# Zeroing in parts on two engines, weights issued first, and dense layers of half-filled tiles on their 64 rows, in a recurrent-memory transformer kernel

## The chip, the cores and the metric

The kernel runs on one core of one Trainium2 chip. The metric is the device time of one execution in microseconds (us). Every timing set runs the kernel before and the other kernel on the same chip. All runs quoted here are of the state that the measurement calls fast.

The engines are called TensorE (PE in the profile; PEld are its weight loads), VectorE (DVE), ScalarE (ACT), GpSimd (POOL) and SyncE (SP). PEclk is the TensorE clock that was granted, as a share of full speed.

## The reference, cut to what matters

```python
x = A_x                                                    # 2048 rows of 512
x = x + _A_ref(_layernorm(x), A_mem0, Wq, Wk, Wv, Wo, 32)  # A: attention over segments with a memory
x = x + _B_ref(_layernorm(x), w1, w2)                      # B: relu(x @ w1) @ w2, 512 -> 1376 -> 512
x = x + _A_ref(_layernorm(x), A_mem0, Wq, Wk, Wv, Wo, 32)
x = x + _B_ref(_layernorm(x), w1, w2)

def _A_ref(x, mem0, Wq, Wk, Wv, Wo, seg_len):
    mem = mem0                                             # 8 rows
    for s in range(64):                                    # one segment of 32 rows after the other
        h = concat([mem, xs])                              # 40 rows
        # q, k, v of 32 heads of 128; masked softmax; o = (p v) Wo
        mem = o[:, :8]                                     # the next segment needs this
        outs.append(o[:, 8:])
```

The memory makes the 64 segments of a layer A sequential. The second layer A can follow the first at a distance.

## The kernel before: the parts that matter

The kernel walks 68 *steps*. In step k it computes segment k of the first layer A and segment k-4 of the second one side by side. After every second step a *pair* (two segments, 64 rows) is finished. Pair j holds the first layers' pair j in rows 0 to 63 of a 128-row tile and the second layers' pair j-2 in rows 64 to 127, and one dense layer works on the whole tile. So of the 34 pairs, pairs 0 and 1 have only the upper half filled, and pairs 32 and 33 only the lower half. The kernel before computes all 128 rows for them all the same.

All work is described as operations with an engine, an estimated cost, what they read and what they write. A list scheduler in the kernel puts them in an order, which is then fixed. The constants RULE and AHEAD shift the priorities in that scheduler. Some operations may go to either of two engines.

```python
def load_weights():
    for i, part in enumerate(("v0", "v2", "q0", "k0", "q2", "k2", "o0", "o2")):
        ...                                    # nc.gpsimd.dma_start of 2 MB each
        plan.op(POOL, 1.0, dma, w=[("W", c, pc), ("W", c, pc + 1)], lag=0.0)

def load_dense():                              # w1 by SyncE, w2 by GpSimd, after the weights ("loaded")
    ...
    plan.op(eng, t, dma, r=["loaded"], w=[w, *[("values", g, p) ...]], lag=10.0)
    # w1_sb and w2_sb hold the values of four groups (EARLY = 4) until these are stored to DRAM (vh)

    # ... prepare():
    def zero_rest():                           # one operation, VectorE alone
        for t in (*Pt, *p_PT.tiles, V0, vw, *p_x.tiles, *p_ox.tiles, *p_xr.tiles, *p_h.tiles):
            nc.vector.memset(t[:], 0.0)

def dense_layer(x, rows):
    xnT = layernorm(x, rows, p_xm)             # VectorE statistics, GpSimd power, VectorE norm, TensorE transpose
    hT = p_h.buf()
    for fb in range((NFC + 3) // 4):           # NFC = 11 chunks of 128 of the 1376 columns
        ...
            for fi, fc in enumerate(fcs):      # first product: 44 weight tiles, 128 columns each
                for c4 in range(NC4):
                    across(cols, hp[0:fs, fi * 128:(fi + 1) * 128], w1_sb[:, c4, fc * 128:fc * 128 + fs],
                           xnT[:, c4, :], start=(c4 == 0), stop=(c4 == NC4 - 1))
        ...                                    # relu into hT
    yp = b_fill.buf()
    ...                                        # second product: 11 matmuls of 512 columns
            across(cols, yp[:, :], hT[0:fs, fc, :], w2_sb[0:fs, fc, :], start=(fc == 0), stop=(fc == NFC - 1))
    return yp

    # ... finish_pair(j), for rows of the second layers:
        def add1():                            # VectorE: the result; then SyncE stores it
            nc.vector.tensor_tensor(out=ob[PR:2 * PR, :], in0=x[PR:2 * PR, :], in1=yp[PR:2 * PR, :], op=ALU.add)

# ... late_values(g): values of 16 rows of each segment of group g, early for g = 1 to 4
        def put():
            nc.sync.dma_start(out=vh[g][:], in_=room[:, :, :])      # 512 KB

prepare()
load_weights()
prepare_group(0)
...
load_dense()
for k in range(nsteps):
    ...                                        # step_values, queries_keys, scores, attend, project
    if k % 2 and k // 2 < NP + D2:
        finish_pair(k // 2)
```

Of the kernel before, what the change touches and what calls it, by code (L numbers as in the profile page):

```python
# [29 lines left out]

RULE = (0.045, 0.734, 51.008, 20.581)
AHEAD = {
    "attend.ev": 0.03, "attend.mm": -1.07, "dense_layer.mm": -0.93, "dense_layer.relu": 1.18,
    "dense_layer.relu_last": -2.98, "finish_pair.add": 2.93, "finish_pair.add0": -0.42, "finish_pair.store": -6.14,
    "finish_pair.turn": 2.99, "finish_pair.widen": 5.86, "late_values.cp": 0.58, "late_values.put": -0.12,
    "layernorm.eps": 0.15, "layernorm.keep": -5.93, "layernorm.norm": 1.95, "layernorm.power": 0.74,
    "layernorm.stats": 0.87, "layernorm.turn": -30.83, "load_dense.dma1": -1.99, "load_dense.dma2": 0.39,
    "load_group.get": 2.78, "load_group.load": -0.5, "load_weights.dma": -3.92, "make_ident": -5.09,
    "make_mask": -0.88, "place_values.dma": -1.35, "prep_x.cp": 3.85, "prepare.get_memory": 0.75,
    "prepare.get_x": 0.11, "prepare.keep": -10.8, "prepare.place": 4.03, "prepare.turn": 5.85,  # L40
    "prepare.zero_banks": 2.29, "prepare.zero_columns": 5.96, "prepare_group.load": 6.09, "prepare_group.put": 0.52,
    "project.ev": 4.4, "project.first": 7.37, "project.mm": -1.19, "queries_keys.ev": 4.38, "queries_keys.mm": -0.14,
    "scores.block": 0.27, "scores.exp": 0.85, "scores.keep": -13.15, "scores.mul": -5.63, "scores.recip": 1.98,
    "scores.sub": -8, "scores.top": 0.05, "scores.total": 20.81, "scores.turn": 1.11, "values.ev": 0.12,
    "values.mm*": -37.11,
}
# [260 lines left out]
def kernel(  # L307
# [74 lines left out]
    def load_weights():  # L382



        for i, part in enumerate(("v0", "v2", "q0", "k0", "q2", "k2", "o0", "o2")):
            c, pc = part[0], int(part[1])

            def dma(c=c, pc=pc):
                if c == "o":  # L390
                    hs = slice(8 * pc, 8 * pc + 16)
                    nc.gpsimd.dma_start(out=Wo_sb[:, hs, :], in_=A_Wo.rearrange("h e d -> e h d")[:, hs, :])
                else:
                    cs = slice(pc * PW, (pc + 2) * PW)
                    nc.gpsimd.dma_start(out=W_s[c][:, :, cs], in_=W_v[c][:, :, cs])

            plan.op(POOL, 1.0, dma, w=[("W", c, pc), ("W", c, pc + 1)], lag=0.0)
            for n in range(2):
                plan.available(("W", c, pc + n), 4.0 + LOAD * (i + 1) + BESIDE * min(i + 1, EARLY + 1))
        plan.available("loaded", 4.0 + LOAD * 8 + BESIDE * (EARLY + 1))  # L400
# [61 lines left out]
    def prepare():  # L462
# [9 lines left out]

        def zero_rest():
            for t in (*Pt, *p_PT.tiles, V0, vw, *p_x.tiles, *p_ox.tiles, *p_xr.tiles, *p_h.tiles):
                nc.vector.memset(t[:], 0.0)

        def get_x():
# [24 lines left out]
        plan.op(DVE, 2.7, zero_banks, w=["banks"])  # L502
        plan.op(DVE, 9.5, zero_rest, w=["zero PT"] + [("vw", p) for p in range(4)] + [("V0", h, b) for h in range(2) for b in range(2)] + [("V0l", b) for b in range(2)] + ["zero x"] + [("P", p, b, x) for p in range(4) for b in range(2) for x in range(2)])
        plan.op(POOL, 0.6, make_ident, w=["ident"])
        plan.op(POOL, 2.3, make_mask, w=["mask"])
# [10 lines left out]
    def layernorm(x, rows, pool, lo=0, n=128):  # L516

        ln, xn, xnT, tp = p_ln.buf(), p_xr.buf(), pool.buf(), b_fill.buf()
        R = slice(lo, lo + n)

        def stats():
# [20 lines left out]
        def keep(eng):  # L542
            copy_on(eng, xnT[:, :, :].rearrange("p c t -> p (c t)"), tp[:, 0:NC4 * n])

# [3 lines left out]
        plan.op(POOL, 0.50, power, r=["mhalf"], w=[ln])  # L548
        plan.op(DVE, 0.50, norm, r=[x, ln, "zero x", *rows], w=[xn])
        plan.op(PE, 0.01 + 1.72e-3 * n, turn, r=[xn, "ident"], w=[tp], tile=EITHER)  # L550
        copy_op(NC4 * n, keep, r=[tp], w=[xnT])
        return xnT

    def dense_layer(x, rows):

        xnT = layernorm(x, rows, p_xm)
        hT = p_h.buf()
        for fb in range((NFC + 3) // 4):
# [3 lines left out]
            def mm(cols=128, hp=hp, fcs=fcs):  # L562
                for fi, fc in enumerate(fcs):
                    fs = 128 if fc < NFC - 1 else F_LAST
                    for c4 in range(NC4):
                        across(cols, hp[0:fs, fi * 128:(fi + 1) * 128], w1_sb[:, c4, fc * 128:fc * 128 + fs],
                               xnT[:, c4, :], start=(c4 == 0), stop=(c4 == NC4 - 1))

            plan.op(PE, 0.23 * len(fcs), mm, r=[xnT, "w1", *([(hT, "own")] if fb else [])],
                    w=[hp] if fb else [hp, hT, (hT, "own")], tile=EITHER if fcs[-1] < NFC - 1 else WHOLE)  # L570
# [7 lines left out]

            def relu(eng, hp=hp, f0=fcs[0], n=nfull):
                relu_on(eng, hT[:, f0:f0 + n, :].rearrange("p f t -> p (f t)"), hp[:, 0:n * 128])  # L580

            def relu_last(eng, hp=hp, n=nfull):
                relu_on(eng, hT[0:F_LAST, NFC - 1, :], hp[0:F_LAST, n * 128:(n + 1) * 128])

            copy_op(128 * nfull, relu, r=[hp, "zero x"], w=[hT, (hT, fb)])
            if nfull < len(fcs):
                copy_op(128, relu_last, r=[hp], w=[hT, (hT, fb)])
        yp = b_fill.buf()
        for fb in range((NFC + 3) // 4):
            fcs = list(range(4 * fb, min(NFC, 4 * fb + 4)))  # L590

            def mm(cols, fcs=fcs):
                for fc in fcs:
                    fs = 128 if fc < NFC - 1 else F_LAST
                    across(cols, yp[:, :], hT[0:fs, fc, :], w2_sb[0:fs, fc, :], start=(fc == 0), stop=(fc == NFC - 1))

            plan.op(PE, 0.216 * len(fcs), mm, r=[hT, (hT, fb), "w2"], w=[yp], tile=EITHER)

        return yp

# [45 lines left out]
    def finish_pair(j):  # L646
# [23 lines left out]
        plan.op(DVE, t_dve(512), add, r=[y, x], w=[("x", j, a) for a in act])  # L670
        yp = dense_layer(x, halves(j))
        if 0 in act:
            x2 = x_tiles[j + D2] = p_x.buf()

            def add0():
                nc.vector.tensor_tensor(out=x2[PR:2 * PR, :], in0=x[0:PR, :], in1=yp[0:PR, :], op=ALU.add)

            plan.op(DVE, t_dve(512), add0, r=[yp, x, ("x", j, 0)], w=[x2, ("x", j + D2, 1)])
            xnT_tiles[(1, j)] = layernorm(x2, [("x", j + D2, 1)], p_xn[1], PR, PR)
        if 1 in act:  # L680
# [3 lines left out]
            def add1():  # L684
                nc.vector.tensor_tensor(out=ob[PR:2 * PR, :], in0=x[PR:2 * PR, :], in1=yp[PR:2 * PR, :], op=ALU.add)  # L685

            def store():
                nc.sync.dma_start(out=out[0, PR * j1:PR * (j1 + 1), :], in_=ob[PR:2 * PR, :])

            plan.op(DVE, t_dve(512), add1, r=[yp, x, ("x", j, 1)], w=[ob])  # L690
            plan.op(SP, 0.78, store, r=[ob], lag=2.45)
# [247 lines left out]
    def project(k, act, seg):  # L939
# [39 lines left out]
        for (j, u), aa in pairs.items():  # L979
# [7 lines left out]

            copy_op(NC4 * SEG * len(aa), rows, r=[wo, "zero x"], w=[ox])

    prepare()  # L990
    load_weights()
    prepare_group(0)
# [69 lines left out]
```

## Time and profile before

| | before |
|---|---|
| time, median of 3 runs | 1683.3 us (1681.63 to 1683.34) |
| the profiled run | 1681.33 us, span 1679.6 us |
| TensorE busy | 97% of the span |
| DMA share, 0 to 60 us | 0.95 (windows view) |
| period of two steps in the steady part | 47.86 us |

Three lines of the page of the kernel before: the span, the busy time of each engine, and the DMA engines' busy tenths in 40 equal slices of 42 us.

```profile
span 1679.6 us, 90364 instructions
PE 1632.9 (97%) x40522; PEld 1396.9 (83%) x40522; DVE 1070.6 (64%) x3095; ACT 1062.2 (63%) x2665; POOL 246.6 (15%) x608
DMA  9621111111110100100010000100010000000000
```

TensorE is full nearly everywhere, and idle for 46.7 us in all (1679.6 less 1632.9). DMA is full only in the first slice and much used in the second. So the two ends of the kernel are what a change can move, besides the amount of TensorE work itself.

**The start.** Lines of the chain of waits before, 56 to 62 us (start, duration, what):

```profile
8.90 48.50 DMA Wo_sb<-in_A_Wo_dram
57.45 0.97 PE st_161 L951 x32
58.42 0.98 PE fill_162 L757 x8
59.41 0.50 PE st_161 L951 x16
```

The end of the weight stream holds step 0: the last half of Wo lands at 57.40 (8.90 + 48.50), and the last projections (st) wait for it. The chunks of eight between them (fill, line 757) are values of a later group that could have run earlier. Next come the first value product (TensorE's timeline) and the stores of early values (SyncE's timeline):

```profile
15.24 1.92 PE L757 MATMUL fill_163<-Wv_sb,HT_80 128*64 128x512 bf16 x8
...
40.87 0.38 SPq L745 DMA_DIRECT2D vh_92<-w_sb  x1
47.14 0.32 SPq L745 DMA_DIRECT2D vh_93<-w_sb  x1
56.93 0.32 SPq L745 DMA_DIRECT2D vh_94<-w_sb  x1
```

**A dense layer in the middle.** One line of the chain before, in step 2: 16 matmuls of the first product take 0.90 us, 56 ns each.

```profile
100.60 0.90 PE fill_163 L514 x16
```

**The last 13.6 us.** Timelines of TensorE and VectorE before (start, duration, engine, line, operation, then the idle time just before it and what ended it):

```profile
1666.04 0.40 PE L514 MATMUL fill_162<-ident,OX_126 128*128 128x128 bf16 x4 [0.36 <-ACT OX_126 L701]
1666.28 2.54 PE L514 MATMUL fill_163<-w_sb,hT_155 128*128 128x512 bf16 x11
1667.20 0.69 DVE L522 BATCH_NORM_STATS2 ln_147<-xg_68 128x6 f32<-128x512 f32 x1
1669.56 0.40 PE L514 MATMUL fill_162<-ident,xr_73 128*128 128x128 bf16 x4 [0.75 <-DVE xr_73 L534]
1670.63 1.05 PE L514 MATMUL fill_163<-xnM_154,w_sb 128*128 128x128 bf16 x16 [0.67 <-ACT xnM_154 L701]
1673.33 2.54 PE L514 MATMUL fill_162<-w_sb,hT_155 128*128 128x512 bf16 x11
```

Pair 33 is alone at the end: transpose of its context, VectorE's normalisation, first product (from 1670.63), second product (from 1673.33), add and store. While VectorE normalises it, TensorE is busy with the second product of pair 32 (the line of 1666.28). Two lines of the windows view before (window, its length, busy us and count of PE, PEld, DVE, ACT, POOL, then PEclk, DMA share, GB/s) show the granted clock at 1.00 to the end of TensorE's work:

```profile
1669.00:1672.00 3.00, 1.76 (x29) 1.69 (x30) 1.20 (x2) 0.81 (x2) 0.00 (x0) 1.00 0.10 22
1672.00:1675.00 3.00, 2.92 (x31) 1.91 (x29) 0.00 (x0) 1.51 (x4) 0.00 (x0) 1.00 0.00 0
```

### The profile page before, as it was taken

Reading aid. Unit: us, or ns where it says so; the run is one execution under the profiler, and the core shown is the slowest. Engines: PE = TensorE matmul, PEld = TensorE weight load, DVE = VectorE, ACT = ScalarE, POOL = GpSimd, SP = SyncE. Lnnn points to the kernel's source line nnn. Section 1 sums busy time; section 2 is a strip of 40 time slices with the busy share of each in tenths; the row PEclk is TensorE's granted clock in tenths of the full one; section 3 lists DMA queues with packets and bytes.
Section 4 is the critical chain, followed back from the end, with each engine's and each line's share of the span. In section 5 each row is a group of like instructions: output and inputs, shape, how many; then the busy total and the mean of one; then the engine's idle time right before and its main releaser. Section 6 shows DMA issues by size and latency. Waiting matters only on the chain.

```text
span 1679.6 us, 90364 instructions
## 1 busy us (share of the span) xinstructions
PE 1632.9 (97%) x40522; PEld 1396.9 (83%) x40522; DVE 1070.6 (64%) x3095; ACT 1062.2 (63%) x2665; POOL 246.6 (15%) x608
## 2 busy tenths in 40 slices
PE   5899999999999999999999999999999999999998
PEld 3678888888888888888888888888888888888886
DVE  5456676676675666676667666666666666766665
ACT  3466666666666666666666666666666666666664
POOL 3111111111111111111111111111111111111110
PEclk9999999999999999999999999999999999999999
DMA  9621111111110100100010000100010000000000
GB/s 358 214 81 35 39 37 28 37 35 37 34 39 16 39 28 17 26 21 24 17 26 20 19 21 19 27 17 25 18 27 16 19 24 21 18 18 18 18 5 6
DMA packets 32500, 64.86 MB, mean 39 GB/s; under 512 B 7048, under 2 KB 16912, under 8 KB 32112
## 3 DMA queue, kind: packets, MB, share of 16 engines
q1 hardware_dynamic: 25984, 39.38, 8.3%
q0 software_dynamic: 4608, 18.19, 2.9%
q8 instruction: 317, 5.19, 1.3%
q10 hardware_dynamic: 1520, 1.52, 0.3%
q14 instruction: 71, 0.58, 0.1%
HBM read 33.89 MB, written 12.45 MB: 28 GB/s over the span
## 4 chain that ended last, share of the span: by engine, by line
PE 81%; DVE 12%; DMA 3%; issue 2%; POOL 1%; ACT 1%; POOLq 0%; ACTq 0%; DVEq 0%
PE st_161 L951 13%; PE fill_162 L757 8%; PE fill_163 L757 8%; PE work_159 L809 7%; PE work_157 L809 7%; PE work_156 L809 7%; PE work_160 L809 7%; PE work_158 L809 6%; PE fill_163 L514 5%; PE fill_162 L514 4%; DMA Wo_sb<-in_A_Wo_dram 3%; DVE OT L703 2%; DVE ob_74 L685 1%; DVE ln_147 L522 1%; POOL P_85 L886 1%
## 5 line engine op out<-in xcount | busy, mean ns | idle before, releaser
L809 PEld LDWEIGHTS <-Wq_sb 128*128 128x128 bf16 x8704 | 333.0, 99 | 30.6 <-issue 13.0
L951 PE MATMUL st_161<-OT,Wo_sb 128*128 128x80 bf16 (+1 forms) x8704 | 354.5, 200 | 2.9 <-DMA Wo_sb<-in_A_Wo_dram 2.9
L951 PEld LDWEIGHTS <-Wo_sb 128*128 128x128 bf16 x8704 | 322.5, 100 | 24.3 <-issue 18.2
L809 PEld LDWEIGHTS <-Wk_sb 128*128 128x128 bf16 x8704 | 335.9, 100 | 4.4 <-DMA Wk_sb<-in_A_Wk_dram 4.4
L701 ACT CAST vw<-fill_162 128x512 bf16<-128x512 f32 x115 | 67.3, 585 | 56.7 <-PE fill_162 L757 52.8
L924 PEld LDWEIGHTS <-vw 128*64 128x64 bf16 (+1 forms) x1536 | 83.7, 107 | 11.8 <-issue 8.3
L701 ACT CAST vw<-fill_163 128x512 bf16<-128x512 f32 x103 | 60.3, 585 | 47.6 <-PE fill_163 L757 43.7
L924 PEld LDWEIGHTS <-V_123 128*64 128x64 bf16 (+1 forms) x1526 | 86.2, 107 | 4.0 <-issue 0.6
L514 PEld LDWEIGHTS <-w_sb 128*128 128x128 bf16 (+1 forms) x1496 | 86.8, 100 | 0.8 <-DVE ob_74 L685 0.5
L757 PEld LDWEIGHTS <-HT_80 128*64 128x64 bf16 x1088 | 51.3, 111 | 32.5 <-issue 2.5
L860 ACT ACTIVATE es_136<-es_136 128x320 f32<-128x320 f32 (+2 forms) x170 | 68.8, 405 | 14.0 <-DVE es_136 L856 9.6
L860 ACT ACTIVATE es_135<-es_135 128x320 f32<-128x320 f32 (+2 forms) x170 | 68.6, 403 | 14.2 <-DVE es_135 L856 6.2
L757 PEld LDWEIGHTS <-HT_81 128*64 128x64 bf16 x1088 | 51.0, 110 | 30.9 <-issue 1.0
L757 PE MATMUL fill_162<-Wv_sb,HT_81 128*64 128x512 bf16 x584 | 76.4, 384 | 0.0
L757 PE MATMUL fill_163<-Wv_sb,HT_80 128*64 128x512 bf16 x544 | 71.9, 387 | 0.0
L757 PE MATMUL fill_162<-Wv_sb,HT_80 128*64 128x512 bf16 x544 | 71.4, 385 | 0.0
L856 DVE TENSOR_TENSOR es_136<-es_136,mx_141 128x320 f32<-128x320 f32 (+2 forms) x170 | 68.9, 405 | 1.0
L853 DVE TENSOR_REDUCE mx_141<-es_136 128x8 f32<-128x320 f32 (+2 forms) x170 | 67.7, 398 | 1.8
L856 DVE TENSOR_TENSOR es_135<-es_135,mx_140 128x320 f32<-128x320 f32 (+2 forms) x170 | 68.0, 400 | 0.9
L853 DVE TENSOR_REDUCE mx_140<-es_135 128x8 f32<-128x320 f32 (+2 forms) x170 | 67.7, 398 | 1.4
L757 PE MATMUL fill_163<-Wv_sb,HT_81 128*64 128x512 bf16 x504 | 66.3, 385 | 0.0
L514 PE MATMUL fill_163<-w_sb,hT_155 128*64 128x512 bf16 (+3 forms) x376 | 54.4, 380 | 0.0
(404 smaller groups left out, 3901.6 us busy)
## 6 DMA issues: line engine op xcount, KB each, us to landing
V_123<-vw SPq DMA_DIRECT2D x252, 48.0 KB
Wv_sb<-in_A_Wv_dram POOLq DMA_DIRECT2D x2, 2048.0 KB, 11.2
Wq_sb<-in_A_Wq_dram POOLq DMA_DIRECT2D x2, 2048.0 KB, 24.2
Wk_sb<-in_A_Wk_dram POOLq DMA_DIRECT2D x2, 2048.0 KB, 29.5
Wo_sb<-in_A_Wo_dram POOLq DMA_DIRECT2D x2, 2048.0 KB, 45.6
out_dram<-ob_74 SPq DMA_DIRECT2D x32, 64.0 KB
w_sb<-in_B_w_dram SPq DMA_DIRECT2D x1, 1376.0 KB
w_sb<-in_B_w_dram POOLq DMA_DIRECT2D x1, 1280.0 KB, 7.4
```

The source lines that it names most:

```text
L514: nc.tensor.matmul(out_[u:v, :], lhsT=lhsT[:, u:v], rhs=rhs, start=start, stop=stop, tile_position=(0, u))
L522: nc.vector.bn_stats(out=ln[R, 0:6], in_=x[R, :])
L685: nc.vector.tensor_tensor(out=ob[PR:2 * PR, :], in0=x[PR:2 * PR, :], in1=yp[PR:2 * PR, :], op=ALU.add)
L701: nc.scalar.copy(out=out_, in_=in_)
L703: nc.vector.tensor_copy(out=out_, in_=in_)
L757: nc.tensor.matmul(vp[64 * b:64 * b + 64, :], lhsT=cols[:, c4, :], rhs=Wv_sb[:, c4, n * 512:(n + 1) * 512], start=(c4 == 0), stop=(c4 == N ...
L809: nc.tensor.matmul(qp[:, hi * 2 * L:hi * 2 * L + n], lhsT=W_sb[:, c4, h * Dh:(h + 1) * Dh], rhs=HT[:, c4, c0:c1], start=(c4 == 0), stop=(c ...
L853: nc.vector.tensor_reduce(out=mx[:, As], in_=es3(), axis=AX.X, op=ALU.max)
L856: nc.vector.tensor_tensor(out=es3(), in0=es3(), op=ALU.subtract, in1=mx[:, As].unsqueeze(2).to_broadcast([128, ns * na, L]))
L860: nc.scalar.activation(out=es[:, A], in_=es[:, A], func=ACTF.Exp, scale=SCALE)
L924: nc.tensor.matmul(o[u:u + cols, :, a, :], lhsT=V[:, p, e0 + u:e0 + u + cols], rhs=PT[:, a, 2 * i + h2, :, :], start=True, stop=True, tile ...
L951: nc.tensor.matmul(wo[:, 2 * W * c4 + c0:2 * W * c4 + c1], lhsT=Wo_sb[:, h, c4 * 128:(c4 + 1) * 128], rhs=OT[:, h, c0:c1], start=(h == 0 a ...
```

## The change

There are four parts.

1. The zeroing is cut into separate operations, each allowed on VectorE or GpSimd, so that the first normalisation need not wait for all of it.
2. The first two weight transfers (both of Wv) are issued before anything else on GpSimd. The other six only stand earlier in the list that the scheduler gets.
3. The dense layer of a pair with one active half works on its 64 rows alone. The first product has 64 columns for each weight tile. The second one is split into two column tiles of 256 columns side by side.
4. RULE and AHEAD have new values, and so the order is a new one.

```diff
-RULE = (0.045, 0.734, 51.008, 20.581)
+RULE = (0.052, 0.937, 39.167, 24.322)
 AHEAD = { ... all values new ... }
-            plan.op(POOL, 1.0, dma, w=[("W", c, pc), ("W", c, pc + 1)], lag=0.0)
+            plan.op(POOL, 1.0, dma, w=[("W", c, pc), ("W", c, pc + 1), *(["issued"] if i < 2 else [])], lag=0.0)
...
-        plan.op(DVE, 9.5, zero_rest, w=["zero PT"] + ... )
-        plan.op(POOL, 0.6, make_ident, w=["ident"])
+        parts = [([t], 0.30, [("P", p, b, x) ...]) for p, t in enumerate(Pt)]
+        parts += [(p_PT.tiles, 1.0, ["zero PT"]), ([V0], 0.92, ...), ([vw], 0.92, ...), (p_xr.tiles, 0.27, ["zero xr"]), ...]
+        for tiles, t, w in parts:
+            def zero(eng, tiles=tiles):
+                for u in tiles:
+                    (nc.gpsimd if eng == POOL else nc.vector).memset(u[:], 0.0)
+            plan.op((DVE, POOL), (t, 1.3 * t), zero, w=w)
+        plan.op(POOL, 0.6, make_ident, r=["issued"], w=["ident"])
...
-    def dense_layer(x, rows):
-        xnT = layernorm(x, rows, p_xm)
+    def dense_layer(x, rows, act):
+        lo, n = PR * act[0], PR * len(act)
+        xnT = layernorm(x, rows, p_xm, lo, n)
...
-                        across(cols, hp[0:fs, fi * 128:(fi + 1) * 128], ..., xnT[:, c4, :], ...)
+                        across(cols, hp[0:fs, fi * n:(fi + 1) * n], ..., xnT[:, c4, lo:lo + n], ...)
...
+                    for u in range(2):
+                        nc.tensor.matmul(yp[64 * u:64 * u + 64, 0:256], lhsT=hT[0:fs, fc, lo:lo + n],
+                                         rhs=w2_sb[0:fs, fc, 256 * u:256 * u + 256], ..., tile_position=(0, 64 * u))
...
+            for u in range(2):                       # add: two of 64x256 in place of one of 64x512
+                cs = slice(256 * u, 256 * u + 256)
+                nc.vector.tensor_tensor(out=to[PR:2 * PR, cs], in0=x[R, cs], in1=yp[64 * u:64 * u + 64, 0:256], op=ALU.add)
...
-    prepare()
     load_weights()
+    prepare()
```

## The prediction

> **What bounds the kernel now.** TensorE. In the windows view it is busy 98.7 us of every 100 from 640 to 1540 us; the chain of waits is 81% TensorE. It is idle 46.7 us of 1679.6 (page, part 1): about 22 us in 0 to 60 us, 2.4 in 60 to 135, 8.5 in 1590 to 1680. Only the two ends can change by much.
>
> **Start.** In the timeline VectorE zeroes until about 8.9 us, then comes the first layernorm; the first value matmul starts at 15.24. GpSimd issues the weights from 1.54 us, after the identity, the last by 10.06; the DMA engines are at 0.95 to 1.0 until 57 us, and the chain's longest piece is the DMA of the last Wo half, 8.90 to 57.40. So DMA throughput bounds the start, not the zeroing.
> - Weights first: the stream starts and ends about 0.9 us earlier.
> - Zeros in parts: the first values come at about 9 us in place of 15.24. This doesn't move the end of the weights. It pays only by moving other work ahead of it: three value chunks of a later group run at 58.35, 59.84 and 61.33 (0.98 us each) between the last projections; if they are done before, step 1 starts up to 2.9 us earlier. Against it: earlier values are stored earlier (512 KB each, 1.3 us of DMA at 370 GB/s) and compete with the weights. Estimate of the whole start: 2 us gained, between 0 and 4.
>
> **Dense layers of 64 rows.** Four pairs of 34 (first two, last two) have one layer active. First product: 44 weight tiles, 56 ns each. The trace gives 36 ns for 80 columns and 25 ns for 40; for 64 I estimate 30 ns. [...] Saved: 1.2 us. Second product: 11 x 512 columns, 215 ns each; now two column tiles of 256, side by side: saved 1.2 us. The transpose saves 0.1. Together 2.5 us of TensorE per pair, 10 for four. Two adds of 64x256 for one of 64x512 (0.69 us) cost about 0.1 us more.
> - Pairs 0 and 1 (from 100 us) lie where TensorE is full: all 5 us count.
> - Pair 33 is the final chain (1666 to 1679.6 us): products 2.5 + 2.5 us halve, copy and last relu shorten by 0.3, adds +0.1: 2.6 us gained.
> - Pair 32: its first product sits between the last projections (1661.4 to 1665.1) and delays them: 1.2 us gained. Its second runs while VectorE normalises pair 33: nothing.
> Sum: about 9 us.
>
> **The order's new constants** move operations in the steady part, where little is left (1.3 us idle per 100): 0 to 1 us gained, with an error of 3 us either way.
>
> **Sum.** 1683.3 - 2 - 9 - 0.8 = about 1671.5 us, 0.7% faster; range 1665.5 to 1677.5. Chances: faster by over 2% 0.02, within 2% 0.97, slower 0.01.
>
> **What would show it.** Timeline: first value matmul near 9 us; last Wo half landing near 56.5; no early value chunks between the projections of step 0. Groups by form: 64-column matmuls at about 30 ns spacing, 64x256 ones in pairs at about 108 ns. From the last context transpose to the end, 13.6 us should become 11. Steady windows stay at 98.7 of 100, the period of two steps at 47.86 us.
>
> **What would make it wrong.** Earlier stores delay the last weights: the start gains nothing. The 64-column form is bound by weight loads (98 ns each, overlapped), spacing over 40 ns: 2 us less. The new order costs or saves more over 68 steps than supposed: 0.1 us per step is 7 us.

The 30 ns for 64 columns stand, as an estimate: a line through the trace's 36 ns for 80 columns and 56 ns for 128 gives 29. The sum: 2 + 9 + 0.8 = 11.8 us.

## The result and the profile after

| | before | after |
|---|---|---|
| median of the first comparison | 1682.47 us (4 runs) | 1678.83 us (4 runs) |
| ratio of that comparison | | 0.9977 [0.9960, 0.9995] |
| repeat in the first set of experiments | 1683.84 us | 1678.53 us, 0.9968 [0.9955, 0.9980] |
| repeat in the fourth set | 1682.19 us | 1678.06 us, 0.9971 [0.9959, 0.9983] |
| profiled run | 1681.33 us, span 1679.6 | 1680.67 us, span 1679.0 |

A ratio is the mean time of one kernel's fast runs over that of the other's of the same rounds, so it is not quite the ratio of the medians. All outputs are right. The kernel gained about 4 to 5.5 us and not the predicted 11.8. It is outside of the range.

A caution on the traces: the only trace before is of a run of 1681.33 us, among its fastest, and the first trace after is of the slowest of its four runs. So one pair of traces shows next to none of the gain (1679.6 against 1679.0). I use three traces of the changed kernel for what follows, and timings for all sums. Two lines of the page after:

```profile
span 1679.0 us, 90465 instructions
PE 1628.4 (97%) x40568; PEld 1395.6 (83%) x40568; DVE 1066.3 (64%) x3090; ACT 1061.1 (63%) x2679; POOL 246.3 (15%) x603
```

TensorE's work fell by 4.5 us only (1632.9 to 1628.4), where the dense layers alone should have taken away 10. Some of it must run slower (the half clock at the end, below).

**Where the time went, step by step.** The end of a step is taken as the start of VectorE's copy of the new memory, which every step has once. The first three columns are ends of steps in us from the start of the span; the last is how much longer or shorter the part became, as the mean of the three traces of the changed kernel less the one trace before.

| part | ends before | ends after (first trace) | mean change of the part |
|---|---|---|---|
| step 0 | 61.43 | 60.31 | -1.49 |
| step 1 | 85.08 | 85.22 | +0.34 (+1.26, +0.08, -0.33) |
| steps 2 to 7 | 228.53 | 226.15 | -2.57 |
| steps 8 to 61 | 1545.54 | 1543.92 | +0.68 |
| steps 62 to 66 | 1647.26 | 1647.53 | +2.00 (1.89, 2.11, 2.00) |
| step 67 and the end | 1679.63 | 1678.97 | -1.20 |

The last column adds up to 2.2 us gained, less than half of what the timings show, because the one trace before is of a fast run. It tells places better than sizes. So the +2.00 of steps 62 to 66 is a high value too: the twelve edited kernels below that keep this order have +0.9 to +1.9 there.

**The start after.** The chain of waits, and then two lines of the timeline (TensorE's and SyncE's):

```profile
13.39 45.06 DMA Wo_sb<-in_A_Wo_dram
58.50 1.78 PE st L974 x64
```

```profile
11.17 2.34 PE L780 MATMUL fill<-Wv_sb,HT 128*64 128x512 bf16 x10
...
30.80 32.26 SPq L768 DMA_DIRECT2D vh<-w_sb  x4
```

The first values come 4.1 us earlier (11.17, not 15.24), though not at 9. The 64 last projections now run in one piece, as predicted. But Wo lands at 58.45, later than before, and not at 56.5. The stores of early values now begin at 30.80 and not at 40.87. Three of the four (30.80, 43.15 and 50.02) are issued well before Wo lands; in the kernel before, two were (40.87 and 47.14), and a third half a microsecond ahead of the landing. Only the two Wv transfers were really put first: GpSimd issues Wq at 7.01 and not at 3.23, and the last half of Wo at 13.39, after layernorm work, not at 8.90. All the zeros stayed on VectorE. The end of step 0 is 1.5 us earlier all the same.

**A dense layer on 64 rows.** The chain after, in steps 2 and 3: 16 matmuls of the first product in 0.54 us (0.47 in pair 32), and 8 of the second one in 0.45 us, where four of 512 columns took 0.87 before.

```profile
103.91 0.54 PE fill L519 x16
116.85 0.45 PE fill L606 x8
1661.73 0.47 PE fill L519 x16
```

The form is what was predicted: 0.47 us for 16 is 29 ns each, and 0.45 us for four side-by-side pairs is 112 ns a pair.

**The end after.** TensorE's and VectorE's timelines:

```profile
1664.90 0.93 PE L606 MATMUL fill<-w_sb,hT 128*64 128x256 bf16 x14
1665.90 0.69 DVE L528 BATCH_NORM_STATS2 ln<-xg 64x6 f32<-64x512 f32 x1
1666.63 0.85 DVE L620 TENSOR_TENSOR ob<-xg,fill 64x256 bf16<-64x256 f32 x2
1669.09 0.42 PE L519 MATMUL fill<-ident,xr 128*64 128x64 bf16 x8 [3.26 <-DVE xr L540]
1669.98 2.78 PE L519 MATMUL fill<-xnM,w_sb 128*64 128x64 bf16 x76 [0.47 <-ACT xnM L724]
1672.69 2.40 PE L606 MATMUL fill<-w_sb,hT 128*64 128x256 bf16 x22
```

The second product of pair 32 is over at 1665.8, before VectorE begins with the statistics of pair 33 (1665.90). TensorE then stands 3.26 us, where it was 0.75 before. Two things opened this gap. The product is halved; and in the new order 8 of its 22 matmuls run before the last context transpose, and VectorE's adds for pair 32 (1666.63) stand in the middle of pair 33's normalisation (before, all eleven matmuls came after the transpose, and the add after the normalisation). The run a_full_last below tells the two apart. And the products of pair 33, with half the columns, take 2.78 and 2.40 us: as long as the full ones before (1670.63 to 1673.33, then 2.54). Windows after:

```profile
1666.00:1669.00 3.00, 0.00 (x0) 0.00 (x0) 2.19 (x6) 0.00 (x0) 0.55 (x1) 0.83 0.09 21
1669.00:1672.00 3.00, 2.44 (x76) 2.29 (x77) 0.04 (x1) 0.76 (x3) 0.00 (x0) 0.50 0.00 1
1672.00:1675.00 3.00, 3.00 (x34) 2.41 (x32) 0.00 (x0) 0.77 (x3) 0.00 (x0) 0.53 0.03 5
```

PEclk is 0.50 and 0.53 where it was 1.00 before. Half the columns at half the clock take the same time. From the last context transpose to the end, which should have become 11 us, it is 14.3 (1664.68 to 1679.0). In the second trace it is 13.5.

**A stand in step 1.** TensorE's waits, 56 to 100 us (who waited, for what: us in total, times, longest), the kernel before and then the changed one:

```profile
PE work_159 L809 <- issue: 1.4, 1, 1.4
```

```profile
PE work L832 <- issue: 2.5, 1, 2.5
```

"issue" means that the profile shows nothing that the engine waited for. The stand was 1.4 us before and is 2.4 to 2.8 us in all three traces of the changed kernel, beginning at 71 to 74 us.

The steady part is nearly as it was: from about step 30 on, most pairs of steps take 47.86 us in both.

### The profile page after: what moved, and what is told of

The parts are those of the page before. It is cut to its first block, busy times and chain, and to the rows that moved or that the text cites. A ratio compares the mean times of both kernels' runs of the same rounds, so it can differ in the third digit from the quotient of the medians.

```text
span 1679.0 us, 90465 instructions
## 1 busy us (share of the span) xinstructions
PE 1628.4 (97%) x40568; PEld 1395.6 (83%) x40568; DVE 1066.3 (64%) x3090; ACT 1061.1 (63%) x2679; POOL 246.3 (15%) x603
## 4 chain that ended last, share of the span: by engine, by line
PE 79%; DVE 13%; DMA 4%; issue 1%; POOL 1%; ACT 1%; SPq 0%; POOLq 0%; DVEq 0%; ACTq 0%
PE work L832 33%; PE fill L780 16%; PE st L974 13%; PE fill L519 8%; PE work L947 3%; PE work L861 3%; DMA Wo_sb<-in_A_Wo_dram 3%; PE work L519 2%; DVE sm L886 2%; DVE OT L726 2%; DVE PT L726 2%; DVE ln L528 1%; DMA V<-vw 1%; POOL P L909 1%; DVE xg L616 1%
## 5 line engine op out<-in xcount | busy, mean ns | idle before, releaser
L832 PE MATMUL work<-HT,Wq_sb 128*128 128x80 bf16 (+1 forms) x8704 | 391.0, 200 | 8.7 <-DVE HT L990 6.7
L832 PE MATMUL work<-HT,Wk_sb 128*128 128x80 bf16 (+1 forms) x8704 | 389.7, 199 | 5.3 <-DMA Wk_sb<-in_A_Wk_dram 2.8
L974 PE MATMUL st<-OT,Wo_sb 128*128 128x80 bf16 (+1 forms) x8704 | 353.6, 200 | 3.7 <-DMA Wo_sb<-in_A_Wo_dram 3.5
L872 DVE TENSOR_TENSOR es<-work,maskb 128x320 f32<-128x320 f32 (+2 forms) x340 | 137.3, 404 | 303.6 <-PE work L861 295.3
L780 PE MATMUL fill<-Wv_sb,HT 128*64 128x512 bf16 x2176 | 282.7, 384 | 0.6 <-DVE vg L726 0.6
L724 ACT CAST qT<-work 128x320 bf16<-128x320 f32 (+1 forms) x500 | 204.6, 409 | 83.7 <-PE work L832 63.3
L724 ACT CAST kT<-work 128x320 bf16<-128x320 f32 (+1 forms) x489 | 200.0, 409 | 74.4 <-PE work L832 29.4
L724 ACT CAST PT<-work 64x320 bf16<-64x320 f32 (+2 forms) x451 | 162.7, 363 | 111.8 <-PE work L519 69.1
L724 ACT CAST OT<-work 128x320 bf16<-128x320 f32 (+1 forms) x374 | 145.1, 409 | 58.7 <-PE work L947 56.9
L883 ACT ACTIVATE es<-es 128x320 f32<-128x320 f32 (+2 forms) x340 | 135.1, 404 | 23.4 <-DVE es L879 13.9
L726 DVE CAST PT<-work 64x160 bf16<-64x160 f32 (+2 forms) x229 | 87.3, 381 | 60.3 <-ACT PT L724 47.0
```

What stands on the lines that cost most here:

```text
L724: nc.scalar.copy(out=out_, in_=in_)
L726: nc.vector.tensor_copy(out=out_, in_=in_)
L780: nc.tensor.matmul(vp[64 * b:64 * b + 64, :], lhsT=cols[:, c4, :], rhs=Wv_sb[:, c4, n * 512:(n + 1) * 512], start=(c4 == 0), stop=(c4 == N ...
L832: nc.tensor.matmul(qp[:, hi * 2 * L:hi * 2 * L + n], lhsT=W_sb[:, c4, h * Dh:(h + 1) * Dh], rhs=HT[:, c4, c0:c1], start=(c4 == 0), stop=(c ...
L872: nc.vector.tensor_tensor(out=flat(es[:, A]), in0=flat(sp[:, A]), op=ALU.add, in1=maskb[:, a_lo:a_hi, :].unsqueeze(2).to_broadcast([128, n ...
L883: nc.scalar.activation(out=es[:, A], in_=es[:, A], func=ACTF.Exp, scale=SCALE)
```

## The experiments

Before the first set I held three theories. Theory C: the end is slow because TensorE falls idle, its clock drops, and the halved products run at half speed. Theory S: the start gains little because the earlier stores hold up the last weights. Theory O: the new order of the constants costs what the parts gain. The rival to all was that the 64-row form itself saves less than estimated. Later a theory L was added for the stand in step 1; the texts call it theory D.

### Set 1: a repeat, and each half of the dense change undone in the same order

**a_again.** The changed kernel, not edited.

> The changed kernel, not edited. It sets the base for the other three of this call and gives a second trace. Ratio to the kernel before 0.9977 as before (0.996 to 0.9995). Theory C (clock): TensorE idles about 4 us after the last projection while VectorE normalises the last pair, the granted clock falls to half, and the last dense layer takes 4.8 us in place of 2.7; so this trace shows a clock near 0.5 in the last 8 us again. Rival F (form): the 64-row form itself costs that time at full clock; then a trace with another clock phase shows the same 4.8 us. Also told apart here: in the first trace TensorE stood 2.5 us at 73.7 us for nothing that the profile shows (kernel before: 1.4 us at 68.75); if that is chance, it differs in this trace.

Measured: 1678.53 us, 0.9968 [0.9955, 0.9980]. The gain is a bit over 5 us here. The clock falls at the end again: PEclk is 0.64 in 1669 to 1672 us, and the two products take 1.98 and 2.56 us.

**a_full_first.** Pairs 0 and 1 compute all 128 rows again. The scheduler is still told the 64-row costs, so the order stays the same.

```diff
-        yp, total, t_total = dense_layer(x, halves(j), act)
+        yp, total, t_total = dense_layer(x, halves(j), act, j in (0, 1))   # full: lo, n = 0, 128; planned costs unchanged
```

> As a_again, same order of operations, but pairs 0 and 1 compute all 128 rows in their dense layers as the kernel before did. My prediction: 2.5 us of TensorE a pair, all on the critical path: 5 us slower than a_again. From the trace of the changed kernel I now expect 4.0 us (the two layers took 4.92 and 4.85 us before, 2.74 and 3.03 after). Rival: TensorE is not what bounds steps 2 to 5 any more, and the time rises by less than 2 us.

Measured: 1682.45 us, 0.9991 [0.9978, 1.0004], so 3.9 us slower than a_again on the same chip. The trace shows the same, 3.87 us by the end of step 8. So the 64-row form of pairs 0 and 1 saves 3.9 us and not 5. The rival that the form saves much less is out.

**a_full_last.** The same for pairs 32 and 33.

```diff
+        yp, total, t_total = dense_layer(x, halves(j), act, j in (32, 33))
```

> As a_again, same order, but pairs 32 and 33 compute all 128 rows. My prediction: 3.8 us slower than a_again. Theory C (clock): the longer second product of pair 32 keeps TensorE busy until VectorE is nearly done, the clock stays at 1.0, so the last layer takes 4.9 us at full clock against 4.8 at half clock: the time rises by only about 1.2 us (0.5 to 1.8), from pair 32's first product between the projections. Rival F: 3.8 us.

Measured: 1680.94 us, 0.9982 [0.9969, 0.9994], so 2.4 us slower than a_again. That lies between the theories (1.2 and 3.8), and what theory C expected of the clock failed: it falls here too, although the second product of pair 32 has its full size again. TensorE's timeline and one window:

```profile
1669.33 0.47 PE L519 MATMUL fill<-ident,xr 128*64 128x128 bf16 x8 [2.41 <-DVE xr L540]
1669.00:1672.00 3.00, 1.99 (x38) 1.85 (x40) 0.28 (x1) 0.58 (x1) 0.00 (x0) 0.59 0.05 11
```

The idle time is 2.41 us, against 0.75 in the kernel before and 3.26 in the changed one. So of the 2.51 us by which it grew, 1.66 are there with full rows in the new order, and the halving adds 0.85. Undoing the halving alone does not bring the clock back. For the size of the gain the run is no clean comparison: its step 67 takes 34.45 us, 2.1 longer than the kernel before with the same rows.

**a_warm.** Fourteen matmuls of 128x512 into an unused bank, to keep TensorE busy over the gap, placed right after the context transpose of pair 33.

```diff
                 across(cols, y[:, c4 * 128:(c4 + 1) * 128], ox[:, c4, :], ident[:])
+            if j == NP + D2 - 1:
+                for i in range(14):
+                    nc.tensor.matmul(b_work.tiles[0][:, :], lhsT=w2_sb[:, 0, 0:128], rhs=w2_sb[:, i % 8, :], start=True, stop=True)
```

> As a_again, with 14 matmuls of 128x512 into an unused PSUM bank (3.0 us at full clock), placed just after the last pair's context transpose, where TensorE otherwise waits 3.9 us for VectorE. Result unchanged. Theory C (clock): the clock stays at 1.0 to the end, the last dense layer takes 2.7 us in place of 4.8, and the time falls by 2 us (1.5 to 2.5) against a_again. Rival F (form): no gain, or 0.1 to 0.5 us lost to the added matmuls.

Measured: 1681.58 us, 0.9982 [0.9969, 0.9996]. This missed, and the fault was in the experiment. The fillers stood *before* the rest of pair 32's second product, so VectorE's adds of pair 32 came only at 1668.82 and pushed pair 33's chain back; a second gap opened and the clock fell anyway (PEclk 0.70 in 1672 to 1675 us). It says nothing against theory C. It does show that those adds sit inside pair 33's chain.

### Set 2: the end and the start apart

**a_warm2.** The same fillers, now after the last matmul of pair 32's second product.

```diff
+                if j == NP + D2 - 2 and fcs[-1] == NFC - 1:
+                    for i in range(14):
+                        nc.tensor.matmul(b_work.tiles[0][:, :], lhsT=w2_sb[:, 0, 0:128], rhs=w2_sb[:, i % 8, :], start=True, stop=True)
```

> As the changed kernel, with the 14 idle matmuls (3.0 us) now placed behind the last matmul of pair 32's second product. In a_warm they stood before it by mistake and held VectorE's add of pair 32, and with it the last chain, 3.6 us longer; so that run told nothing of the clock. Theory C (clock): the last layer of pair 33 runs at clock 1.0: its two products take about 2.7 us in place of 4.1 to 4.8, and the time is 1.3 to 2.2 us lower than the changed kernel's (1678.5 us: 1676.3 to 1677.2). Rival F (form): within 0.3 us of 1678.5.

Measured: 1676.40 us, 0.9962 [0.9950, 0.9975]. TensorE's timeline and one window of the trace:

```profile
1664.28 3.20 PE L611 MATMUL work<-w_sb 128*128 128x512 bf16 x14
1667.61 0.32 PE L519 MATMUL fill<-ident,xr 128*64 128x64 bf16 x8
1668.39 1.74 PE L519 MATMUL fill<-xnM,w_sb 128*64 128x64 bf16 x76 [0.47 <-ACT xnM L727]
1670.12 1.39 PE L606 MATMUL fill<-w_sb,hT 128*64 128x256 bf16 x22
```

```profile
1669.00:1672.00 3.00, 2.51 (x71) 2.16 (x65) 0.39 (x1) 1.15 (x4) 0.00 (x0) 1.00 0.02 5
```

Useless work made the kernel's end faster. The clock stays at 1.00, the first product takes 1.74 us and not 2.78, the second 1.39 and not 2.40. Step 67 takes 29.32 us, against 31.44, 30.70 and 31.38 in the three traces without fillers. Theory C is shown by this: the half clock made the last products long, and work in the gap prevents it. In timings the step from a_again's ratio to this one is 1.0 us, from the later repeat's 1.5; these are across sets, and small against the interval.

**a_addlate.** The adds and the store of pair 32 are moved behind the normalisation of pair 33 in the fixed order.

```diff
+    late = [marks["add", NP + D2 - 2], marks["store", NP + D2 - 2]]
+    ops = [o for o in ops if o not in late]
+    at = ops.index(marks["norm"]) + 1
+    ops[at:at] = late
```

> As the changed kernel, with one move: VectorE's two adds and the store that end pair 32 stand behind the normalisation of pair 33 in place of between its statistics. The last chain of VectorE should be 0.7 to 0.85 us shorter, so TensorE idles 3.2 us before the last layer in place of 3.9 to 4.2: 0.8 us faster than the changed kernel if the clock stays as it is; up to 2.5 us faster if the shorter gap also keeps the clock up (Theory C). If the chain of VectorE didn't bound the end: no change.

Measured: 1677.38 us, 0.9968 [0.9955, 0.9980]. The idle time shrank from 3.26 to 2.49 us, but the clock fell all the same (PEclk 0.50 in 1666 to 1672 us). The gain is within the noise: shortening VectorE's chain a little does not save the clock.

**a_warm_addlate.** Both.

> Both edits. Theory C: 2 to 3 us faster than the changed kernel (1675.5 to 1676.5 us), the last 14 us at clock 1.0, and the tail from the last projection to the end about 2.6 us shorter than in the kernel before, as I had predicted. The 3.0 us of idle matmuls may now end after VectorE and cost up to 0.3 us.

Measured: 1675.87 us, 0.9957 [0.9943, 0.9970]; step 67 takes 29.17 us. Against a_again's ratio that is 1.9 us.

**a_putlate.** The four stores of early values (512 KB each) are issued after step 0, by ScalarE.

```diff
-            nc.sync.dma_start(out=vh[g][:], in_=room[:, :, :])
+            (nc.scalar if 1 <= g <= EARLY else nc.sync).dma_start(out=vh[g][:], in_=room[:, :, :])
...                                             # and in the fixed order:
+    at = ops.index(marks["rows", 0]) + 1
+    for o in puts:
+        ops.insert(at, o)
+        at += 8
```

> As the changed kernel, but the four early stores of values (512 KB each) are issued by ScalarE after it has copied step 0's result, so that none of them moves while the weights are still coming. My prediction named their contention as a cost of 1.3 us each. If it holds: the last Wo half lands 2.5 to 4 us earlier than 58.4 us, step 0 ends 2 us earlier (1 to 3), and the time falls as much. If DMA of the weights is bound by something else than the shared throughput: no change in the landing.

Measured: 1677.39 us, 0.9967 [0.9954, 0.9979]. The chain and the waits of its trace:

```profile
13.40 41.44 DMA Wo_sb<-in_A_Wo_dram
```

```profile
PE work L947 <- DMA V<-vw: 2.9, 1, 2.9
```

Wo lands at 54.84 and not at 57.9 to 58.5, and step 0 ends at 56.70 and not at 59.7 to 60.3. So theory S is right in its mechanism: the stores hold the weights up by about 3 us. The time does not show it: the ratio is that of a_again. Step 1's own transfers (V from vw) now run behind the stores and the loads of the dense weights, and TensorE waits 2.9 us for them, in place of the stand of 2.4 to 2.8 us. But the trace doesn't show that this hands the gain back: step 1 takes 24.66 us (24.90, 23.72 and 23.31 in the changed kernel) and ends at 81.36, still 1.8 to 3.9 us ahead of the three traces (85.22, 83.44 and 83.12). The five timings spread from 1675.26 to 1680.55 us, so they don't settle how much of it lasts.

### Set 3: the order taken apart from the parts

**a_oldconst** is the changed kernel with the old RULE and AHEAD. **b_newconst** is the kernel before with the new ones. **b_dense** and **b_start** are the kernel before with the dense change alone (diff part 3) and with the start alone (parts 1 and 2), both with the old constants. In each the scheduler deals a new order.

```diff
-RULE = (0.052, 0.937, 39.167, 24.322)          # a_oldconst; b_newconst is the reverse on the kernel before
+RULE = (0.045, 0.734, 51.008, 20.581)
 AHEAD = { ... likewise ... }
```

> The changed kernel with the order's constants of the kernel before: all of the new work, another order. My prediction took 0 to 1 us for the new constants. Against the kernel before, step by step, the changed kernel lost about 1.3 us of order in steps 2 to 7, 1.0 in steps 8 to 61 and 2.1 in steps 62 to 66. Theory O (order): these come from the new constants; with the old ones the steady part is as in the kernel before and the time is 1 to 3 us lower than the changed kernel's. Rival: the new order earns at the two ends what it loses between; the time is 2 us or more higher.

Measured: 1681.93 us, 0.9990 [0.9978, 1.0002].

> The kernel before with the new constants alone. Theory O: slower than before by 1 to 4 us, with the loss in the steady part and in steps 62 to 66. Rival: the same within 1 us.

Measured: 1686.54 us, 1.0011 [0.9996, 1.0025].

> The kernel before with the 64-row dense layers alone (start and constants as before). My prediction: 8.8 us faster than before. With what the other runs showed: 3.9 us from pairs 0 and 1, and of the last two pairs 1 to 3.5 by what the clock does: 5 to 7 us faster.

Measured: 1686.01 us, 1.0009 [0.9997, 1.0021].

> The kernel before with the new start alone (zeros in parts, weights first; constants and dense layers as before). My prediction: 2 us faster, 0 to 4. The changed kernel's two traces show step 0 ending 1.1 and 1.7 us earlier, so 1 to 2 us faster.

Measured: 1679.44 us, 0.9974 [0.9961, 0.9986].

Theory O in its simple form falls. The new constants are worth about 3 us on the new operations (a_oldconst against the repeats), although on the old operations they are worth nothing, or a loss of 2. The trace of b_newconst, with all 128 rows everywhere, shows a part of such a loss: its order puts the whole second product of pair 32 before the last context transpose, TensorE then stands 3.51 us, and the first product of pair 33 takes 4.74 us (2.7 before, waits within it included) at PEclk 0.50 in 1674 to 1677 us:

```profile
1672.32 0.60 PE L513 MATMUL fill<-ident,xr 128*128 128x128 bf16 x4 [3.51 <-DVE xr L533]
1673.60 4.74 PE L513 MATMUL fill<-xnM,w_sb 128*128 128x128 bf16 x44 [0.67 <-ACT xnM L700]
```

So the order alone can lose the clock at the end, without any 64-row layer. And theory O's core stands in another form: the order answers to every change. The dense change alone gained *nothing*, where undoing half of it in a fixed order cost 3.9 us. The trace of b_dense shows the time lost in the steps that should gain: step 4 ends at 154.97 us, against 151.68 before, and the last layer runs at PEclk 0.53 and 0.50 (1674 to 1680 us) after a gap of 3.19 us; there, too, all of pair 32's second product came before the transpose. b_start gained 4.4 us by its ratio, twice what I had given the start, yet its trace (of its slowest run) shows step 0 only 0.35 us shorter and step 1 2.4 us shorter; much of its gain lies beyond the mechanism that I predicted. Taken alone, the parts do not add up to the whole: 0.9974 and 1.0009 against 0.997.

### Sets 4 and 5: the stand in step 1, and a version that keeps the gains

Still open after set 3: why a_putlate's 3 us don't show in the time, and what the "issue" stand there is. Theory L: both loads of the dense weights (1376 KB each) are now issued within two microseconds, at 64.9 to 66.7 us in the second repeat; in the kernel before the first goes at 63.02 and the other after 80 us. They fill the DMA engines (share 1.02 in 70 to 75 us of the first trace), and everything that step 1 needs by DMA comes late.

**a_third.** The changed kernel again.

> The changed kernel once more, as the base of this call: 1677.5 to 1679.5 us.

Measured: 1678.06 us, 0.9971 [0.9959, 0.9983]. Stand in step 1: 2.4 us.

**a_all1.** a_warm_addlate and a_putlate together.

> The changed kernel with three edits: idle matmuls before the last layer, the adds of pair 32 after the last normalisation, and the four early stores after step 0 as in a_putlate. If the causes add up: 2.6 us (tail) and 1 to 2 us (start) less than a_third: 1674 to 1675 us. If the start's gain is always given back: 1676.

Measured: 1675.61 us, 0.9954 [0.9942, 0.9966]. It gains as a_warm_addlate does. Against that kernel's trace step 0 ends 2.7 us earlier and step 1 only 0.6: here step 1 does give most of it back, with a wait of 3.6 us for the same transfers.

**a_all2.** As a_all1, but the stores and the loads of the dense weights all stand behind step 1's transfers of values.

```diff
+    at = max(ops.index(o) for o in (marks["rows", 0], *marks["copies"])) + 1
+    for o in (*puts, *loads):
+        ops.insert(at, o)
+        at += 3
```

> As a_all1, but the stores and the dense weights' loads come after step 1's copies of values have been issued, so step 1 has no large transfer ahead of them. If the 2.9 us wait of step 1 in a_putlate came from the stores: step 1 waits under 0.5 us, and the time is 1 to 2 us below a_all1: 1672.5 to 1674 us, about what I had predicted for the changed kernel. Rival: the wait comes from something else, or the late loads of the dense weights hold pair 0: no better than a_all1.

Measured: 1679.03 us, 0.9979 [0.9967, 0.9991], a miss. TensorE's longest wait and GpSimd's timeline:

```profile
PE fill L784 <- POOL XG L760: 4.5, 1, 4.5
```

```profile
77.59 1.02 POOL L406 DMA_DIRECT2D w_sb<-in_B_w_dram  x1 [8.10 <-DMA vh<-w_sb]
```

The load of w2 may start only when the values parked in its space have been stored. It stood ahead of other work in GpSimd's fixed order, GpSimd waited 8.10 us for those stores, and TensorE waited 4.5 us for a copy that GpSimd had to do after it. Here, a DMA issue that had to wait held up all that stood behind it on its engine.

**a_loadlate.** The unedited changed kernel, but both loads of the dense weights stand behind step 1.

```diff
+    loads = [marks["dense", n] for n in range(2)]
+    ops = [o for o in ops if o not in loads]
+    at = ops.index(marks["rows", 1]) + 1
+    ops[at:at] = loads
```

> The changed kernel with one move: both dense weight loads are issued after step 1's result has been copied (about 84 us) in place of 65 to 67 us. Theory D (DMA backlog): the stand of 2.4 to 2.8 us at 73 us goes, step 1 is about 2 us shorter, and the time is 1.5 to 2.5 us below the changed kernel's. Rival N (no link): TensorE stands there as before and the time is unchanged. If the loads now come too late for pair 0 at about 100 us, the stand moves there.

Measured: 1676.18 us, 0.9956 [0.9943, 0.9968]. First one window of the kernel before, then the same of a_third, then that of a_loadlate with a later window and TensorE's longest wait between 56 and 100 us (which lies at 86.2 to 88.1):

```profile
70.00:75.00 5.00, 4.86 (x78) 2.78 (x78) 2.53 (x10) 2.05 (x6) 0.32 (x1) 0.66 0.01 3
```

```profile
70.00:75.00 5.00, 2.61 (x94) 2.39 (x91) 2.15 (x11) 2.31 (x9) 0.93 (x3) 0.97 1.02 343
```

```profile
70.00:75.00 5.00, 4.66 (x157) 4.21 (x155) 4.21 (x19) 3.85 (x15) 1.89 (x7) 1.00 0.33 86
85.00:90.00 5.00, 3.11 (x102) 2.66 (x100) 1.18 (x5) 2.03 (x8) 0.31 (x1) 1.00 0.89 308
```

```profile
PE work L832 <- issue: 1.9, 1, 1.9
```

With the loads, the DMA share in 70 to 75 us is 1.02 and TensorE is busy for 2.61 of 5 us. Without them it is 0.33, TensorE is busy for 4.66, and step 1 takes 19.75 us (23.3 in a_third). And the stand moved *with* the loads: in 85 to 90 us, where they now run, TensorE has a stand of 1.9 us that it had not there before. So in these two traces the stand lies where the loads fill the DMA engines (1.02 and 0.89); that is shown. In the kernel before, the shorter stand (68.75 to 70.14 us) comes just after such a stretch: the share is 1.05 in 66 to 68 us, 0.51 in 68 to 69 and 0.19 in 69 to 70. In the repeats a stretch of lower clock follows the stand (PEclk 0.66 and 0.69 in 75 to 80 us), which a_loadlate is spared as well (1.00 from 75 to 95 us, its own stand included); the kernel before has one too (0.66, first line). Not all of it is won: steps 2 to 7 take 142.89 us, 2.1 longer than in a_third, so about 1.5 of the 3.6 us are left by the end of step 7. By ratios, across two sets, the gain is 2.0 to 3.5 us with overlapping intervals.

What TensorE lacks in the stand the views don't say. I suspect its instructions: the profile's page lists two DMA queues of kind "instruction", and all 317 packets of the larger one before (q8, 5.19 MB) are of 16 KB. That it is TensorE's I infer from its size: it moves 5.19 of the 5.77 MB of the two, and TensorE has 81044 of the 90364 instructions. No run here tests it, but the packets in the kept traces speak for it. Sixteen of them have 17 stands of over 0.9 us put down to "issue" after the first 20 us, and in each one TensorE goes on 1.3 to 1.6 us after a packet of q8 has landed. In the kernel before the packet lands at 68.78 us and TensorE goes on at 70.14; in the first trace after it is 74.71 and 76.24. In a_third the packet runs from 71.21 to 72.36 us and the stand from 71.53 to 73.91. These packets come about once in 5 us, so that is hardly chance. In a_third it is not slower than the others (1.15 us, median 1.06): what came late would be their start, and why is not shown.

**a_all3.** a_loadlate with the fillers and the late adds. **a_all4.** a_all3 with the late stores of a_putlate as well.

> a_loadlate with the two edits of the tail (idle matmuls, late adds). Theory D: 1.5 to 2.5 us below a_warm_addlate's ratio of 0.9957 to the kernel before, that is 0.9943 to 0.9948, about 1673 to 1674 us. Rival N: 0.9957.

Measured: 1674.86 us, 0.9949 [0.9937, 0.9962].

> a_all3 with the early stores after step 0 as well. Theory D: step 0 ends 2.5 to 3 us earlier and step 1 waits at most 1 us for its copies behind the stores alone, so the gain of the stores is kept at last: 1671 to 1673 us, about what I had predicted for the changed kernel. Rival: the stores alone hold step 1's copies for 2.5 us or more: no better than a_all3.

Measured: 1672.21 us (1670.74 to 1674.84), 0.9932 [0.9919, 0.9945]. Within one set that is 1676.18, 1674.86, 1672.21: the end's repair 1.3 us by medians, the late stores 2.7. The time fell where it was expected, but the traces don't show the expected way: against a_all3 step 0 ends 2.23 us earlier (57.48 and 59.71), and step 1 only 0.58 (78.89 and 79.47; 85.22 in the changed kernel). Step 1 has no wait for its copies now, but PEclk is 0.76 and 0.90 in 55 to 65 us, where a_all3 has 1.00. So the early end of step 1 is the work of the moved loads, and how much of the 2.7 us is due to the late stores stays open; the intervals of the two ratios overlap. This version beats both kernels. It adds 14 matmuls whose result nobody reads, and moves eight operations in the fixed order. It was not tried what the same moves would do for the kernel before.

## Why the prediction was wrong

The bound was right: TensorE is full in the steady part (640 to 740 us: busy 98.73 us before, 98.51 after), and only the ends moved. The sum was wrong: 11.8 us predicted, 4 to 5.5 measured. Here are its terms.

- **"Pairs 0 and 1 ... all 5 us count."** The mechanism was right, and so was the spacing (29 ns measured, 30 estimated). The term was mis-sized: in a fixed order it is 3.9 us (a_full_first). In the step table only 2.57 us of it arrive in steps 2 to 7, as the new order spends part: a_full_first, with all rows in this order, takes 1.30 us longer there than the kernel before.
- **"Pair 33 ... 2.6 us gained", "Pair 32 ... 1.2 us gained. Its second runs while VectorE normalises pair 33: nothing."** This step failed. I took the second product of pair 32 as work that costs nothing because it hides behind VectorE. It did something: it kept TensorE busy. Halved, and in the new order begun before the last transpose, it leaves 3.26 us of idle TensorE right before the last layer, which then runs at PEclk 0.50. The whole gain of pair 33's products is lost to that. By a_full_last the order has the larger part in the gap (1.66 us, the halving 0.85). Step 67, which holds both pairs' share, gained 1.2 us in place of 3.8; in the fixed order the two pairs are worth 2.4 us (a_full_last, where the clock fell too). With the clock held up (a_warm2) step 67 takes 29.32 us, 3.05 less than before, so most of the 3.8. At this place in the traces a lower clock follows the longer idle times: after a stand of 3.26 us, with 0.47 more after a short transpose, PEclk was 0.50 (0.64 in the window of a_again), and it was 0.50 after 2.49 us in a_addlate; after 2.41 us in a_full_last it was 0.59 in the window shown; after 0.75 and then 0.67 us, in the kernel before, it stayed at 1.00. A safe length the traces don't give: in step 1 the stand of 1.4 us before was followed by 0.66 (70 to 75 us), that of 1.9 us in a_loadlate by 1.00. I had not asked how long a gap the change would open here, nor what clock would follow it.
- **The start, "2 us gained, between 0 and 4".** The direction was right, and the named danger (earlier stores delay the last weights) came true: the three stores in the stream cost about 3 us (a_putlate), near the 1.3 us each that I had counted. But the kernel before had two of them in the stream already, so against it the last weights land only up to 1 us later. "The stream starts and ends about 0.9 us earlier" failed: the first weights start only 0.2 us earlier (1.34 and not 1.54), the other six transfers are issued later than before, and the last weights land at 57.85 to 58.45 us (57.40 before). Step 0 gained 1.5 us since the three value chunks moved out of its end, and step 1 gave 0.3 of that back on average. Those are traces; by timings b_start gained 4.4 us, which is more than I can assign.
- **"The order's new constants ... 0 to 1 us gained, with an error of 3 us."** This is the largest shortfall. With 3.9 for the first pairs, 2.4 for the last and about 1.2 for the start, 7.5 us should have been gained; about 5 were. The step table shows where some 2.5 us went: up to 2.0 into steps 62 to 66, where a_oldconst loses 0.5, and 0.7 into steps 8 to 61. The new order's constants are none the less better than the old ones on these operations. What I missed is that *new operations* mean a new order, constants or not. It was as a part of that order that both loads of the dense weights fell together into step 1, with a stand that costs 2.4 to 2.8 us (1.4 before). The prediction never looked at step 1, where a slice with a DMA tenth of 6 was in plain sight.

So the sizes that failed are about 1.1 us for the first pairs, 1.4 for the last, 0.8 for the start and 3.3 for the order, 6.6 in all against a shortfall of 6.4 to 6.9 by the repeats. The order's 3.3 is only what the other terms leave, so that this sum agrees by construction and checks nothing; and with the 1.2 us that step 67 gained in the traces the last pairs would miss 2.6, and the order less. This bookkeeping mixes timings with traces and leans on sets of different rounds, each with an interval of about 2 us either way; I hold it for fair in its order of size, not for exact.

A check on it: repairing the three named losses (the clock at the end, the stores in the weight stream, the loads in step 1) gave 1672.21 us. That is near the predicted 1671.5, but it is no proof that these were the prediction's losses: some of the repairs remove waits that the kernel before had as well.

Three things stay open: what makes steps 62 to 66 longer in the new order, what delays TensorE's instructions in the stand of step 1 (if it is they), and how much the late stores are worth.

## What to carry to other kernels

Before you shorten work that "hides behind" another engine, ask what it hides: near the end of a kernel it may be all that keeps TensorE's clock up (here a gap grew from 0.75 to 3.26 us, and PEclk fell from 1.00 to 0.50 after it), so look at the length of the idle gap that the cut leaves and at PEclk after it, and check that a new order leaves that work where it hides the wait. A kernel whose order comes from a scheduler answers to every edit with a new order, so test a part by undoing it in a *fixed* order, and expect some microseconds from the re-dealing alone (a_oldconst: about 3). When a transfer is made to end earlier, look at what the next stage needs from the DMA engines: the late stores brought the end of step 0 forward by 2.7 us in a_all1 and 2.2 us in a_all4, and in both the end of step 1 by only 0.6.
